# Two attention layers on one core: who rounds off B's v weights, and when the v stage's inputs are asked for

## The chip, the cores and the metric

The kernel runs on one core of one Trainium2 chip. The metric is the device time of one execution in microseconds (us); the median of three runs of the kernel before is 1763.21 us (1762.25 to 1763.91).

## The reference, cut to what matters

Two independent attention layers A and B read inputs of 2048 rows by 640 columns and share no data; their results stand side by side in the output.

```python
# both: H = 32 heads of Dh = 20, float32
qkv = (x @ wqkv).reshape(B, S, 3, H, Dh)          # q, k, v
# A: each row looks at itself and 7 earlier rows, 2 apart (W = 8, dil = 2)
logits = einsum("bhsd,bhswd->bhsw", q, kg) * scale ; attn = softmax(logits)
o = einsum("bhsw,bhswd->bhsd", attn, vg) ; a = o @ wo
# B: full attention, every row with every row
p = softmax(einsum("bhqd,bhkd->bhqk", q, k) * scale)
o = einsum("bhqk,bhkd->bhqd", p, v) ; b = o @ wo
return concatenate([a, b], axis=-1)
```

## The kernel before, in words

**Two parts for every operand.** TensorE multiplies rounded float32. To keep accuracy, each operand of a projection is split in two (`split`): a *first part*, the rounded value (ScalarE, ACT in the profile), and a *second part*, what rounding lost, by one subtraction (VectorE, DVE, unless another engine is passed as `second`). A product is three passes: first by first, first weight by second x, second weight by first x. So a matmul group can't begin its third matmul before the second part of its weights is there.

**Stages.** (1) A's q and k projections. (2) B's q and k projections: five loops over `m`, each with eight groups of 15 matmuls; the last one (`m == 8`, groups 0 to 7) is where the first inputs of the next stage are asked for. (3) The *v stage*: the v projections of A and then of B, in 15 blocks of four row tiles. x is held in eight columns (c = 0 to 3 of A, 4 to 7 of B) and the weights in two halves, so block 2c + half takes column c and one half. Blocks 0 and 1 are eight plain groups. From block 2 on a block is four *ticks*: 30 half-height matmuls for v and then four for one step of B's row maxima (`b_max`, scores into two PSUM pairs, each read by a VectorE maximum over 1024 columns). There are 52 such steps (`LEAD`). (4) The *loop*: 488 steps of B's attention, in which TensorE computes scores twice (transposed ones for the exponentials by ScalarE, plain ones for later maxima by VectorE) and multiplies by v. Its order is written out by hand in the string `ORDER`: S, Y, M and N are pairs of score matmuls with the PSUM banks they use, V ends a step, H is a piece of A's output projection, j a transposition for A. (5) 24 last steps without maxima, and B's output projection.

**A's attention** runs on GpSimd (POOL in the profile) beside all this, as a generator that hands out a few instructions per tick. `a_pace` lets it run until a running sum of estimated GpSimd time, `gp.us`, reaches a target; every `tensor_` operation given to `gp` adds to that sum, whoever gave it. The loop sets the sum to 0 and goes on at 2.4 us a step.

**What sets the order.** Each engine runs its own instructions in the order in which the program writes them; a waiting instruction holds up all behind it. All loads and stores named here are issued by SyncE (SP), in order. Buffers rotate: a load waits until the earlier use of its buffer is over. `stg` has three (weights before splitting), `p` six (x before splitting, and the B projections' results `pr` on their way to memory), `big` four (x columns, and `bk`, `bq`, the k and q of one group of B's heads), `w` four.

**The requests.** `wait[0]` holds after how many ticks a loaded piece is split. `x_pieces(xa, 0)` asks for x's first column of the v stage; `x_load(c, w)` for the later ones, with second parts by GpSimd; `wide_pieces(wv_a[1])` for A's second weight half, and `w_load(half, w)` for B's halves: half 0 after block 4, split nine ticks later (block 7's first tick), half 1 inside block 7, split four ticks later (block 8's second tick). In the profile these tiles are called `xn` and `xl` (x, four of five row chunks and the last), `ww` (weights), `stg` (what was loaded), `ro` (A's v on the way out), `ve` (B's), `mx` (maxima), `al`, `am`, `akv`, `aq`, `ao` (A's attention). Nearly every instruction shows line 71, that of a helper, so rows are told apart by tile.

## Time and profile before

| What | Value |
|---|---|
| Median of three runs | 1763.21 us |
| The profiled execution's own time | 1762.02 us |
| Its span, first to last instruction | 1760.2 us |
| Busy: TensorE, VectorE, ScalarE, GpSimd | 1734.1, 1357.8, 1338.2, 1265.9 us |
| Mean granted TensorE clock | 0.991 of full |

The span leaves 1.8 us of the execution's own time outside it. Stage 3 reaches from 280.85 us to about 469 us, the loop from there to about 1642 us. "Busy" of TensorE counts overlapping, modelled matmuls, so 99% says only that it rarely stood still for long; what a stage costs is read from the starts of its matmuls.

### The profile page before, as it was taken

How to read it: one execution, taken by the hardware profiler on the slowest of the kernel's cores; microseconds unless marked ns; L12 is line 12 of the kernel's file. 1: busy time of each engine (PE TensorE's matmuls, PEld its weight loads, DVE VectorE, ACT ScalarE, POOL GpSimd, SP SyncE). 2: the span in 40 equal slices, each digit the busy share in tenths (PEclk: the TensorE clock that was granted, in tenths of full speed). 3: DMA queues.
4: the chain of work that ended last, by engine and by line, in shares of the span. 5: the costliest groups of instructions: out<-in, count | busy, mean ns of one | idle time of the engine just before them, and what ended most of it. 6: DMA issues, size and time to landing. Idle time of an engine off the chain costs nothing.

```text
span 1760.2 us, 34683 instructions
## 1 busy us (share of the span) xinstructions
PE 1734.1 (99%) x12711; PEld 1014.8 (58%) x12711; DVE 1357.8 (77%) x1816; ACT 1338.2 (76%) x2658; POOL 1265.9 (72%) x1119
## 2 busy tenths in 40 slices
PE   9999998989999999999999999999999999999999
PEld 8988887979834544444354444444434444444569
DVE  3113232798899999999999999999989999999300
ACT  4223223231499999999999999999989999999881
POOL 0001940988899999999999999999999934544242
PEclk9999999999999999999999999999999999999999
DMA  6447868665755355445436344553553432111123
GB/s 224 121 142 251 301 224 273 210 200 168 207 175 136 110 128 163 129 116 152 138 110 154 115 135 114 168 157 103 141 151 116 119 83 58 44 36 52 33 71 115
DMA packets 194436, 248.29 MB, mean 141 GB/s; under 512 B 89309, under 2 KB 114397, under 8 KB 193273
## 3 DMA queue, kind: packets, MB, share of 16 engines
q1 hardware_dynamic: 193688, 245.41, 46.1%
q8 instruction: 100, 1.64, 0.4%
q10 hardware_dynamic: 576, 0.66, 0.1%
q14 instruction: 72, 0.58, 0.1%
HBM read 181.08 MB, written 64.91 MB: 140 GB/s over the span
## 4 chain that ended last, share of the span: by engine, by line
PE 77%; POOL 13%; DVE 5%; DMA 2%; ACT 2%; issue 2%; POOLq 0%; SPq 0%; DVEq 0%; ACTq 0%
PE ps_st L71 77%; POOL akv L71 7%; DVE mx L71 4%; POOL braw L71 3%; ACT e L71 1%; POOL ao L71 1%; DMA qb_d<-pr 1%; DVE ww L71 1%; POOL aot L71 1%; POOL al L71 0%; POOL ro L71 0%; DMA stg<-wv_a 0%; DMA stg<-xa 0%; DMA tr_d<-turn 0%; ACT more L71 0%
## 5 line engine op out<-in xcount | busy, mean ns | idle before, releaser
L71 DVE TENSOR_REDUCE mx<-ps_st 128x1 f32<-128x512 f32 (+1 forms) x1492 | 1226.7, 882 | 69.7 <-PE ps_st L71 58.8
L71 ACT ACTIVATE e<-ps_st 128x512 f32<-128x512 f32 x2048 | 1068.1, 629 | 33.5 <-PE ps_st L71 21.1
L71 PE MATMUL ps_st<-bk,bq 60*128 60x512 f32 x2048 | 561.8, 440 | 11.6 <-DVE mx L71 10.7
L71 PE MATMUL ps_st<-bq,bk 62*128 62x512 f32 x2048 | 548.2, 432 | 1.4 <-ACT e L71 1.3
L71 PE MATMUL ps_st<-e,vb 128*32 128x512 f32 x4096 | 545.0, 607 | 0.6
L71 PEld LDWEIGHTS ps_st<-bq,bk 62*128 62x128 f32 x2048 | 276.7, 185 | 402.8 <-ACT e L71 272.5
L71 POOL TENSOR_TENSOR braw<-braw,more 128x512 f32<-128x512 f32 x224 | 288.2, 1286 | 99.6 <-ACT more L71 99.0
L71 PEld LDWEIGHTS ps_st<-bk,bq 60*128 60x128 f32 x2048 | 258.3, 185 | 114.2 <-DVE mx L71 73.3
L71 POOL TENSOR_TENSOR akv<-akv,aq 128x1280 f32<-128x1280 f32 x64 | 188.5, 2945 | 166.2 <-DMA akv<-ka_d 166.1
L71 POOL TENSOR_TENSOR akv<-akv 128x640 f32<-128x640 f32 (+3 forms) x304 | 282.4, 929 | 14.9
L71 ACT COPY ro<-ps_st 128x320 f32<-128x320 f32 (+2 forms) x172 | 73.8, 465 | 190.3 <-PE ps_st L71 99.0
L71 PE MATMUL ps_st<-ww,xn 64*128 64x320 f32 (+1 forms) x1776 | 191.7, 315 | 7.4 <-ACT ww L71 4.8
L71 PEld LDWEIGHTS ps_st<-ww,xn 64*128 64x128 f32 (+1 forms) x1776 | 179.9, 192 | 24.2 <-ACT e L71 8.3
L71 PEld LDWEIGHTS ps_st<-e,vb 128*32 128x32 f32 x4096 | 82.5, 108 | 150.6 <-issue 76.8
L71 POOL TENSOR_TENSOR akv<-akv,al 128x1280 f32<-128x1280 f32 x64 | 151.5, 2367 | 0.1
L71 ACT COPY more<-ps_st 128x512 f32<-128x512 f32 x224 | 136.7, 610 | 4.0 <-PE ps_st L71 3.3
L71 PE MATMUL ps_st<-xn,w 128*128 128x512 f32 x480 | 115.8, 390 | 0.0
L71 POOL TENSOR_TENSOR xn<-stg,xn 128x512 fp32r<-128x512 f32 (+1 forms) x30 | 54.9, 1841 | 70.2 <-DMA va_d<-ro 62.9
L71 PEld LDWEIGHTS ps_st<-xn,w 128*128 128x128 f32 x480 | 90.1, 188 | 19.3
L71 PE MATMUL ps_st<-ww,aot 64*128 64x320 f32 x960 | 99.6, 309 | 0.0
L71 ACT CAST pr<-ps_st 128x512 fp32r<-128x512 f32 x40 | 23.5, 587 | 97.9 <-PE ps_st L71 95.0
L71 PEld LDWEIGHTS ps_st<-ww,aot 64*128 64x128 f32 x960 | 90.5, 186 | 4.9 <-issue 0.9
(65 smaller groups left out, 1046.0 us busy)
## 6 DMA issues: line engine op xcount, KB each, us to landing
akv<-ka_d SPq DMA_DIRECT2D x128, 320.0 KB
akv<-va_d SPq DMA_DIRECT2D x128, 320.0 KB
kb_d<-pr SPq DMA_DIRECT2D x20, 512.0 KB
qb_d<-pr SPq DMA_DIRECT2D x20, 512.0 KB
bk<-kb_d SPq DMA_DIRECT2D x16, 640.0 KB
bq<-qb_d SPq DMA_DIRECT2D x64, 160.0 KB
stg<-xb SPq DMA_DIRECT2D x16, 512.0 KB
rb<-s_d SPq DMA_DIRECT2D x128, 64.0 KB
```

The costliest lines, as they stand in the source:

```text
L71: return self.tc.keep_in_program_order(op(*a, **k))
```

## The change

Four edits, and a new `ORDER`:

- `w_load` passes GpSimd for the second parts of B's v weights; the first parts stay on ScalarE. Six VectorE instructions go, six GpSimd instructions come.
- x's first column is asked for in the loop `m == 6`, group 4, instead of `m == 8`, group 1: five groups sooner. It is split at the same tick as before (ten ticks after the request, not five).
- A's second weight half is asked for after group 3 of `m == 8`, not after group 7: four groups sooner, split at the same tick (seven, not three).
- x's second column is asked for after the first v group, not the second, and split one tick sooner.
- The `ORDER` string is another one throughout, with as many steps, H and j; S, Y, M and N are 627, 698, 444 and 127, where they were 619, 714, 452 and 111.

```diff
-    def wide_pieces(src, second=None):
+    def wide_pieces(src, second=None, first=None):
...
-            w[0][:, a:b], w[1][:, a:b], src[:, a:b], second=second, first=second and gp.tensor_copy) for a, b in PAIRS]
+            w[0][:, a:b], w[1][:, a:b], src[:, a:b], second=second, first=first or second and gp.tensor_copy) for a, b in PAIRS]
...
+                elif m == 6 and (n, j) == (2, 0):
+                    wait[0] = 10
+                    XV = [x_pieces(xa, 0)]
+                    for fn in XV[0][1]:
+                        fn()
+                    wait[0] = 2
                 elif m == 6 and (n, j) == (3, 0):
                     w0, loads = wide_pieces(wv_a[0])
                 elif m == 8:
                     g8 = 2 * n + j
                     if g8 == 1:
                         k_loads, q_loads = b_pieces(0)
-                        wait[0] = 5
-                        XV = [x_pieces(xa, 0)]
-                        for fn in XV[0][1]:
-                            fn()
                     elif 1 < g8 < 6:
                         k_loads.pop(0)()
+                        if g8 == 3:
+                            wait[0] = 7
+                            w1, more = wide_pieces(wv_a[1])
+                            for fn in more:
+                                fn()
                     elif g8 == 6:
                         for _ in range(4):
                             q_loads.pop(0)()
-                    elif g8 == 7:
-                        wait[0] = 3
-                        w1, more = wide_pieces(wv_a[1])
-                        for fn in more:
-                            fn()
...
-        WV[1][half], pieces = wide_pieces(wv_b[half])
+        WV[1][half], pieces = wide_pieces(wv_b[half], gp, act.copy)
...
-                if (block, s) == (0, 1):
+                if (block, s) == (0, 0):
                     x_load(1, 5)
...
-        "Y07S61M2Y45V0Y71S26M3Y05V7Y06M3S52Y71V0Y26M3S75VY71M5S24S03N17V2Y06S15Y34VM0S74Y56V3Y70S21N46VY70M4S12S63N07V1"
+        "Y07M1S36Y54V0Y71S26M4Y03V7Y06M4S31Y72V0Y13M4S76VY71M2S64S05N17V6Y04M2S51VY70M4S13S26N07V1Y25S04N36VY07S25M3Y61"
```

On SyncE, at the end of stage 2, the loads of A's second weight half (`stg<-wv_a`, its last three rows) stood so before, behind the last two of the first four loads of q (`bq`) and the last store of B's projections (`qb_d<-pr`):

```order
L71 DMA bq<-qb_d 20x1024
L71 DMA bq<-qb_d 40x1024
L71 DMA qb_d<-pr 128x2x512
L71 DMA stg<-wv_a 128x640 x2
L71 DMA stg<-wv_a 128x320
```

Now they stand so, right behind the second of the four loads of k (`bk`):

```order
L71 DMA bk<-kb_d 40x4096
L71 DMA qb_d<-pr 128x2x512
L71 DMA bk<-kb_d 22x4096
L71 DMA stg<-wv_a 128x640 x2
L71 DMA stg<-wv_a 128x320
```

The three loads have passed two loads of k, four of q and four stores of `pr`.

On GpSimd, in block 7, behind the x column of block 8 (`xn`, `xl`), A's attention (`akv`, `al`) came next before:

```order
L71 TENSOR_TENSOR xn<-stg,xn 128x1024 x2
L71 TENSOR_TENSOR xl<-stg,xl 128x512
L71 TENSOR_TENSOR akv<-akv 128x2x320
L71 TENSOR_TENSOR akv<-akv 128x2x160
L71 TENSOR_TENSOR akv<-akv 128x2x64
```

Now the two weight halves (`ww`) are there as well:

```order
L71 TENSOR_TENSOR xl<-stg,xl 128x512
L71 TENSOR_TENSOR ww<-stg,ww 128x640 x2
L71 TENSOR_TENSOR ww<-stg,ww 128x320
L71 TENSOR_TENSOR akv<-akv 128x2x320
L71 TENSOR_TENSOR akv<-akv 128x2x160
L71 TENSOR_TENSOR akv<-akv 128x2x64
L71 TENSOR_TENSOR akv<-akv 128x2x32
L71 TENSOR_TENSOR al<-akv 128x64
L71 TENSOR_TENSOR al<-al,am 128x256
L71 TENSOR_TENSOR akv<-akv,aq 128x1280
L71 TENSOR_TENSOR ww<-stg,ww 128x640 x2
L71 TENSOR_TENSOR ww<-stg,ww 128x320
```

Half 0 follows directly on the x column of block 8; half 1 comes after one more piece of A's attention, and ahead of block 10's column.

On VectorE, in blocks 5 to 9, the maxima (`mx`) had the two weight halves and a reciprocal for A (`am`) between them, and now follow one another:

```order
-L71 TENSOR_REDUCE mx_3092<-ps_st 128x2 x8
-L71 TENSOR_TENSOR ww<-stg,ww 128x640 x2
-L71 TENSOR_TENSOR ww<-stg,ww 128x320
-L71 TENSOR_REDUCE mx_3092<-ps_st 128x2 x10
-L71 TENSOR_TENSOR ww<-stg,ww 128x640 x2
-L71 TENSOR_TENSOR ww<-stg,ww 128x320
-L71 TENSOR_REDUCE mx_3092<-ps_st 128x2 x10
-L71 RECIPROCAL am<-am 128x32
-L71 TENSOR_REDUCE mx_3092<-ps_st 128x2 x2
+L71 TENSOR_REDUCE mx_3092<-ps_st 128x2 x30
```

Six subtractions have left VectorE, and the reciprocal comes later.

## The prediction

> **What bounds the kernel now.** I read the busy times first, then TensorE's own waits, then the starts of its matmuls where it waited, then what the named releasers did.

> ```profile
> PE 1734.1 (99%) x12711; PEld 1014.8 (58%) x12711; DVE 1357.8 (77%) x1816; ACT 1338.2 (76%) x2658; POOL 1265.9 (72%) x1119
> PE ps_st L71 <- DVE mx L71: 10.7, 7, 4.6
> PE ps_st L71 <- ACT ww L71: 4.8, 1, 4.8
> PE ps_st L71 <- POOL xn L71: 2.6, 2, 1.4
> ```

> The first row is busy time by engine, the others TensorE's waits (total, times, longest). TensorE hardly stands still: 18 us in three kinds of wait. Two of the kinds, and 7 of the 10.7 us behind the maxima, lie in the v stage, which is what the change touches. There TensorE alone sets the pace, so a wait counts in full, and more, as the starts of its matmuls show:

> ```profile
> 280.85 1.92 PE L71 MATMUL ps_st<-ww,xn 128*128 128x320 f32 x12
> 283.05 1.92 PE L71 MATMUL ps_st<-ww,xn 128*128 128x320 f32 x12
> ...
> 294.65 3.90 PE L71 MATMUL ps_st<-ww,xn 128*128 128x320 f32 x12 [4.83 <-ACT ww L71]
> ...
> 306.07 0.41 PE L71 MATMUL ps_st<-ww,xn 64*128 64x320 f32 x2
> ...
> 313.34 1.92 PE L71 MATMUL ps_st<-ww,xn 64*128 64x320 f32 x24
> ...
> 367.37 1.92 PE L71 MATMUL ps_st<-ww,xn 64*128 64x320 f32 x24
> ...
> 370.08 1.93 PE L71 MATMUL ps_st<-ww,xn 64*128 64x320 f32 x24
> ...
> 377.09 0.80 PE L71 MATMUL ps_st<-bk,bq 60*128 60x512 f32 x2 [4.64 <-DVE mx L71]
> ...
> 378.82 3.16 PE L71 MATMUL ps_st<-ww,xn 64*128 64x320 f32 x24
> ...
> 382.72 1.93 PE L71 MATMUL ps_st<-ww,xn 64*128 64x320 f32 x24
> ...
> 390.84 1.92 PE L71 MATMUL ps_st<-ww,xn 64*128 64x320 f32 x24
> ...
> 397.14 3.40 PE L71 MATMUL ps_st<-ww,xn 64*128 64x320 f32 x24
> ...
> 402.00 1.95 PE L71 MATMUL ps_st<-ww,xn 64*128 64x320 f32 x24
> ```

> An undisturbed group takes 283.05 - 280.85 = 2.20 us, an undisturbed tick 370.08 - 367.37 = 2.71. Against these, four places lose time:

> - A: blocks 0 and 1, eight groups from 280.85 to 306.07, take 25.22 where 8 x 2.20 = 17.6 would do: 7.6 lost, for a wait of 4.83. The rest is a slow clock: twelve matmuls take 3.90 behind the wait, not 1.92.
> - B: block 2's first tick, 306.07 to 313.34, takes 7.27, not 2.71: 4.6 lost, 2.6 of it waiting for x's second column.
> - C: from 370.08 to 382.72, two ticks take 12.64, not 5.42: 7.2 lost.
> - D: from 390.84 to 402.00, two ticks take 11.16: 5.7 lost.

> Together 25.1 us. This is what the change can win in the v stage, no more.

> **The change, part by part.** *A's second weight half, four groups sooner (place A).*

> ```profile
> 269.07 0.41 SPq L71 DMA_DIRECT2D bk<-kb_d  x1
> 285.72 3.66 SPq L71 DMA_DIRECT2D stg<-wv_a  x3
> 293.87 0.72 ACT L71 CAST ww<-stg 128x640 fp32r<-128x640 f32 x1 [7.99 <-DMA stg<-wv_a]
> 304.34 2.00 ACT L71 CAST xn<-stg 128x1024 fp32r<-128x1024 f32 x2
> 305.48 4.69 POOL L71 TENSOR_TENSOR xn<-stg,xn 128x1024 fp32r<-128x1024 f32 x2 [62.95 <-DMA va_d<-ro]
> 310.11 1.30 POOL L71 TENSOR_TENSOR xl<-stg,xl 128x512 fp32r<-128x512 f32 x1
> 250.00:265.00 15.00, 15.00 (x67) 12.36 (x67) 4.75 (x7) 4.68 (x8) 0.00 (x0) 1.00 0.62 209
> 265.00:312.00 47.00, 39.57 (x219) 35.41 (x219) 9.77 (x14) 13.26 (x24) 6.44 (x5) 0.90 0.83 271
> ```

> The loads are issued from 285.72 on and the first is rounded at 293.87, 8.15 us later, on queues that are 83% busy (last row: stretch, length, busy TensorE, its loads, VectorE, ScalarE, GpSimd, clock, DMA share, GB/s). Block 1 wants the weights at 280.85 + 4 x 2.20 = 289.65. Now they are issued behind the second load of k (269.07): about 269.5, and by the same 8.15 they are there at 278, some 8 us before ScalarE comes to them. The wait and its slow clock go: **-7.6**. Bounds: -4.8 (the clock stays slow) to -7.6; 0 if the loads don't come sooner (a rival).

> What the moved loads cost. The first load of k now waits longer, since x's column has taken the buffer that k had, and k gets that of the next B column: until group 3 of `m == 8` is done. Stores and the weights queue behind it on SyncE, for 1 to 2 us; TensorE has results in eight banks to write before that reaches it, so I cost it at nothing. x's first column goes from the busy stretch to the one before it (62% busy). Its three `p` buffers are held five groups longer, as they were from 265 to 280 before, without a wait of TensorE. Without that cover each late store would cost one group at most, 3.4 us.

> *x's second column, one group sooner (place B).* GpSimd begins at 305.48, behind ScalarE at 304.34, and ends at 311.4 (310.11 + 1.30); block 2 begins at 306.07. One group is 2.20 us, so against block 2 the column is ready 2.20 sooner: of the waits of 2.6, about 1.5 remain by the order of need (the second piece ends 1.0 late, the last 0.4). Behind a wait the clock stays slow: at C this cost 382.72 - 378.82 - 2.71 = 1.2, which I take. Lost 2.7 instead of 4.6: **-1.9** (0 if the load lands 2 us late, -4.6 at best). That the whole border is 1.31 MB lighter (x's first column has left it; at 271 GB/s 4.8 us) speaks for the load being in time.

> *B's weights by GpSimd (places C and D).*

> ```profile
> 369.60 6.30 DVE L71 TENSOR_TENSOR ww<-stg,ww 128x640 fp32r<-128x640 f32 x3
> 390.36 3.86 DVE L71 TENSOR_TENSOR ww<-stg,ww 128x640 fp32r<-128x640 f32 x3
> 265.16 0.83 DVE L71 TENSOR_TENSOR ww<-stg,ww 128x640 fp32r<-128x640 f32 x1
> 369.66 5.90 POOL L71 TENSOR_TENSOR xn<-stg,xn 128x1024 fp32r<-128x1024 f32 x2
> 376.99 3.41 POOL L71 TENSOR_TENSOR akv<-akv 128x640 f32<-128x640 f32 x4
> 381.44 2.96 POOL L71 TENSOR_TENSOR akv<-akv,aq 128x1280 f32<-128x1280 f32 x1
> L71 POOL TENSOR_TENSOR ww<-stg,ww 128x640 fp32r<-128x640 f32 x8 | 12.5, 1559 | 0.6
> L71 POOL TENSOR_TENSOR ww<-stg,ww 128x320 fp32r<-128x320 f32 x4 | 3.5, 872 | 0.3
> 395.00:400.00 5.00, 4.25 (x26) 3.65 (x28) 3.76 (x4) 1.40 (x2) 4.99 (x3) 0.52 0.15 53
> ```

> Before, VectorE takes 6.30 and 3.86 us for the halves, and the maxima behind them keep TensorE's banks: places C and D. Both go. What is late next is GpSimd: a half costs 2 x 1.56 + 0.87 = 4.0 us there. In the clock of the old trace: x's column for block 8 begins at 369.66 and, without VectorE beside it, takes 4.69 as at 305.48, and 1.30: 375.65. The pieces of half 0 end at 377.2, 378.8 and 379.6. Block 8 would begin at 370.08 + 2 x 2.71 = 375.5 and wants the first piece 0.3 later, the second 0.9 behind the first (30 matmuls in 2.20): waits of 1.4 and 0.7, then the slow clock, 1.2. C loses 3.3 instead of 7.2: **-3.9** (0 if GpSimd is 3 us later than in the old trace, -7.2 if TensorE is).

> Half 1: GpSimd does 7.4 us of A's work first (376.99 to 384.40), so its pieces end at 388.6, 390.1 and 391.0. Block 9 begins at 375.5 + 3.3 + 4 x 2.71 = 389.6 and wants them at 389.9, 390.5 and 391.4: in time, by half a microsecond. I leave 0.5 lost: **-5.2** (-2 to -5.7). SyncE, in turn, waits with half 1's loads until GpSimd frees `stg`, 3.7 us later than VectorE did; stores of A's v and the next x column are behind it, and both have a block's time. Later x columns have 4 us or more left on GpSimd by the same count.

> [...]

> *The loop.* It has the same matmuls, exponentials and maxima, differently paired.

> ```profile
> 468.00:1640.00 1172.00, 1167.12 (x8671) 531.41 (x8670) 1134.67 (x1577) 1133.29 (x2270) 1014.36 (x894) 1.00 0.42 120
> L71 DVE TENSOR_REDUCE mx<-ps_st 128x2 f32<-128x1024 f32 x556 | 671.9, 1217 | 42.7 <-PE ps_st L71 40.2 <-ACT e L71 0.5
> L71 DVE TENSOR_REDUCE mx<-ps_st 128x1 f32<-128x512 f32 x936 | 606.4, 683 | 26.9 <-PE ps_st L71 18.6
> DVE am L71 <- POOL al L71: 6.3, 3, 2.2
> 1310.00:1320.00 10.00, 7.35 (x44) 2.60 (x44) 7.62 (x10) 5.84 (x13) 9.76 (x10) 0.83 0.42 124
> ```

> VectorE and ScalarE are both busy for 97% of it, so it is their work that counts. M takes one maximum over 1024 (1.217), N two over 512 (0.683 each), Y one. Eight M fewer, 16 N more, 16 Y fewer: -9.7 + 21.9 - 10.9 = **+1.2**. GpSimd, which gave 8.0 us of the v stage to weights, does as much of A's attention later; it has room, since it is busy for 1014 of 1172 us. A new order can't win more than VectorE's idle 37 us; what it does to waits no row shows. I take none, and -4 to +8 for it.

> **Sum:** -7.6 - 1.9 - 3.9 - 5.2 + 1.2 = -17.4. The profiled execution's own 1762.02 becomes 1744.6; it lies 1.2 under the median of 1763.21, from which the forecast is **1745.8 us**.

> **The rivals.** *GpSimd bounds the v stage.* If it falls behind by 3 us more, C and D are given back almost whole, and B too: only A is won. 1763.2 - 7.6 + 1.2 = 1756.8. For it: GpSimd's work there grows by 8.0 while 17 us of TensorE's waits, in which it caught up, go. Against it: `a_pace` counts the weights and hands out less of A's work. [...] 0.12.

> *A's weights don't come sooner,* since SyncE is held by the load of k, or the queues stay full. A stays: 1745.8 + 7.6 = 1753.4. Against it: 8 us of slack. 0.06.

> *Slower: GpSimd's delay reaches VectorE in the loop.* At 1311 us VectorE waits 2.2 us for A's scores (`am` for `al`), and ScalarE loses 10 - 5.84 = 4.2 us between 1310 and 1320, while GpSimd is 98% busy. A's softmax comes 16 times; each further one that finds GpSimd late costs 4.2. From five on (1745.8 + 21 = 1766.8) the kernel is slower. Any other flaw of the new order that delays one step in a hundred by as much does the same. Against it: only three of 16 waited before, and the count of H and j falls two to three steps later in the new order, about the 8 us. 0.14, at 1768.

> *Better:* the stall at 1311 goes and the clock holds: 1745.8 - 4.2 - 2.4 = 1739. 0.10.

> **How the numbers follow.** Forecast 0.58, with its own range of 1741 to 1752; rivals 0.12, 0.06, 0.14, 0.10. From 1737 to 1759 some 0.82 of the chance lies; left out are the slower case and the ends. Within 0.2% (1759.7 to 1766.7, about what a measurement of this kernel can tell from no change) lie the near misses of two rivals: 0.07. Faster 0.80, slower 0.13.

> **What would show it.** Right: no wait for `ww` on ScalarE near 290; no wait for `mx` on TensorE in the v stage, but two of about 1 us for GpSimd's `ww` at block 8; the loop's first step some 18 us sooner than 469; 488 steps in 1172 to 1175 us. Wrong: waits for `xn` or `ww` of GpSimd over 3 us at blocks 8 to 14; a loop longer by over 8 us; more than three waits of `am` for `al`.

## The result, and the profile after

| | before | after |
|---|---|---|
| Median of four runs each | 1763.12 us | 1744.71 us (1743.93 to 1746.89) |
| Ratio, 95% interval | | 0.9898 (0.9881 to 0.9915): 1.0% less time, clear of the noise |
| Profiled execution, own time | 1762.02 us | 1745.1 us |
| Its span | 1760.2 us | 1742.9 us |
| Loop's first score matmul at | 468.95 us | 454.27 us |
| From there to the last stage (the loop) | 1175.20 us | 1173.76 us |
| The rest of the span | 116.05 us | 114.87 us |

The forecast of 1745.8 is 1.1 us from the median. That hides errors of about 5 us on opposite sides, which the rows below show.

Busy time by engine, after:

```profile
PE 1726.1 (99%) x12711; PEld 1011.2 (58%) x12711; DVE 1349.3 (77%) x1818; ACT 1337.3 (77%) x2658; POOL 1271.9 (73%) x1125
```

VectorE has 8.5 us less to do, GpSimd 6.0 more; neither sum says where the end moved. TensorE's waits over the whole span do (total, times, longest):

```profile
PE ps_st L71 <- ACT xn L71: 2.6, 2, 2.2
PE ps_st L71 <- POOL xn L71: 2.4, 2, 2.0
PE ps_st L71 <- DVE mx L71: 2.0, 5, 0.6
PE ps_st L71 <- POOL ww L71: 1.9, 3, 1.2
PE ps_st L71 <- ACT e L71: 1.8, 1, 1.8
```

The 4.8 us for ScalarE's `ww` are gone. The 10.7 behind VectorE's maxima are 2.0, all of them in the loop. New are 1.9 for GpSimd's `ww`, 2.6 for ScalarE's `xn` (2.2 of it in the v stage), of which no row of the profile before spoke, and 1.8 in one wait for ScalarE's `e`, in the loop. Where they lie is seen from TensorE's matmuls in the v stage (start, length, in brackets the idle time ahead and what ended it); the last two rows are the loop's first score matmul and the first matmul behind its end:

```profile
281.15 1.92 PE L71 MATMUL ps_st<-ww,xn 128*128 128x320 f32 x12
...
296.55 1.92 PE L71 MATMUL ps_st<-ww,xn 128*128 128x320 f32 x12
...
301.12 0.41 PE L71 MATMUL ps_st<-ww,xn 64*128 64x320 f32 x2 [2.21 <-ACT xn L71]
...
303.56 1.97 PE L71 MATMUL ps_st<-ww,xn 64*128 64x320 f32 x12 [2.02 <-POOL xn L71]
...
309.03 1.96 PE L71 MATMUL ps_st<-ww,xn 64*128 64x320 f32 x24
...
371.21 0.46 PE L71 MATMUL ps_st<-ww,xn 64*128 64x320 f32 x4
372.90 1.14 PE L71 MATMUL ps_st<-ww,xn 64*128 64x320 f32 x12 [1.23 <-POOL ww L71]
374.41 0.85 PE L71 MATMUL ps_st<-ww,xn 64*128 64x320 f32 x8 [0.37 <-POOL ww L71]
...
376.02 1.92 PE L71 MATMUL ps_st<-ww,xn 64*128 64x320 f32 x24
...
384.12 1.33 PE L71 MATMUL ps_st<-ww,xn 64*128 64x320 f32 x16
385.72 0.87 PE L71 MATMUL ps_st<-ww,xn 64*128 64x320 f32 x8 [0.27 <-POOL ww L71]
...
387.32 1.92 PE L71 MATMUL ps_st<-ww,xn 64*128 64x320 f32 x24
...
454.27 0.51 PE L71 MATMUL ps_st<-bq,bk 62*128 62x512 f32 x1
...
1628.03 1.92 PE L71 MATMUL ps_st<-e,vb 128*32 128x512 f32 x16
```

Read with the undisturbed 2.20 us a group and 2.71 a tick:

| Place | Lost before | Lost after | Change | Predicted |
|---|---|---|---|---|
| A, blocks 0 and 1: 296.55 - 281.15 = 7 x 2.20 | 7.6 | 0 | -7.6 | -7.6 |
| B, block 2's first tick: 309.03 - 298.75 - 2.71 | 4.6 | 7.6 | **+3.0** | -1.9 |
| C, block 8's first tick: 376.02 - 371.21 - 2.71 = 2.10 | 7.2 | 2.1 | -5.1 | -3.9 |
| D, block 9's first tick: 387.32 - 384.12 - 2.71 = 0.49 | 5.7 | 0.5 | -5.2 | -5.2 |
| Start of the stage: 280.85 became 281.15 | | | +0.3 | 0 |
| Loop, and the rest of the span (-1.4, -1.2) | | | **-2.6** | +1.2 |

(298.75 is where block 2 would begin: 296.55 + 2.20.) The rows of the table sum to -17.2; the span is 17.3 shorter.

Place B has got worse. What ScalarE did ahead of it, after:

```profile
294.37 0.43 ACT L71 COPY ro<-ps_st 128x320 f32<-128x320 f32 x1 [3.80 <-DMA va_d<-ro]
299.70 0.43 ACT L71 COPY ro<-ps_st 128x320 f32<-128x320 f32 x1 [4.90 <-DMA va_d<-ro]
300.02 1.99 ACT L71 CAST xn<-stg 128x1024 fp32r<-128x1024 f32 x2
```

ScalarE stands still for 3.80 and 4.90 us before a row copy (`ro`): it waits for the store of an earlier row (`va_d<-ro`) to free one of four row buffers. Behind the second copy, in ScalarE's order, stands the rounding of x's second column, at 300.02, though block 2 wanted it at 298.75. GpSimd's second parts follow only then, from 301.15. Before, with TensorE at rest at A and the stores going out meanwhile, ScalarE's last copy ahead of the column waited for TensorE only:

```profile
304.02 0.42 ACT L71 COPY ro<-ps_st 128x320 f32<-128x320 f32 x1 [1.78 <-PE ps_st L71]
304.34 2.00 ACT L71 CAST xn<-stg 128x1024 fp32r<-128x1024 f32 x2
```

So ScalarE, held by the store of a row, is the first wait at B, and GpSimd's second parts, which come after it, are the second. The stores did not move with the groups: SyncE issued the second row's store at 292.57 us, and before at 292.13, though its row was copied by 286.2 in both. SyncE issues in order, and ahead of that store stand two loads of q and the x column, the first of which was issued only at 289.62, after a wait of 3.2 us that the profile puts down to k's DMA (`bk`).

Two stretches of the loop, 200 us each, the first two rows of before, the other two of after (stretch, length, busy TensorE, its loads, VectorE, ScalarE, GpSimd, clock, DMA share, GB/s):

```profile
470.00:670.00 200.00, 199.85 (x1514) 96.12 (x1512) 194.22 (x285) 190.82 (x385) 189.11 (x168) 1.00 0.52 146
1270.00:1470.00 200.00, 196.66 (x1488) 90.34 (x1486) 190.86 (x266) 190.06 (x381) 159.82 (x135) 0.99 0.40 114
470.00:670.00 200.00, 197.08 (x1500) 91.21 (x1492) 193.12 (x280) 190.46 (x383) 191.97 (x172) 1.00 0.49 140
1270.00:1470.00 200.00, 199.83 (x1526) 93.98 (x1522) 196.39 (x278) 193.50 (x388) 158.34 (x135) 1.00 0.40 109
```

Before, the second stretch held the stall near 1311, and TensorE was busy for 3.2 us less in it than now: that stall is gone. In the first stretch TensorE is now busy for 2.8 us less. Most of this is one wait: ScalarE can't copy a partial result of B (`more`) until GpSimd has added an earlier one (`braw`), and TensorE then waits 1.85 us for ScalarE's `e`.

```profile
490.49 0.58 ACT L71 COPY more<-ps_st 128x512 f32<-128x512 f32 x1 [1.98 <-POOL braw L71]
```

The two nearly cancel. The loop's -1.4 is no more than the scatter: with the old `ORDER` and the same order of instructions the loops of before, e1 and e9 (below) take 1175.20, 1173.05 and 1174.54 us, and the seven kernels with the new `ORDER` in which `gp.us` counts B's weights take 1172.87 to 1174.89. The 1.2 us of the rest of the span come from a slow clock in before's profiled execution (0.50 of full from 1644.49 to 1647.90): there the second group of sixteen matmuls behind the loop starts 7.15 us after the first (1644.15, 1651.30), and in after 5.50.

### The profile page after: what moved, and what is told of

It is laid out like the page before. It is cut to its first block, busy times and chain, and to the rows that moved or that the text cites. A ratio compares the mean times of both kernels' runs of the same rounds, so it can differ in the third digit from the quotient of the medians.

```text
span 1742.9 us, 34666 instructions
## 1 busy us (share of the span) xinstructions
PE 1726.1 (99%) x12711; PEld 1011.2 (58%) x12711; DVE 1349.3 (77%) x1818; ACT 1337.3 (77%) x2658; POOL 1271.9 (73%) x1125
## 4 chain that ended last, share of the span: by engine, by line
PE 73%; POOL 17%; DMA 4%; issue 3%; DVE 2%; ACT 1%; SPq 1%; POOLq 0%; ACTq 0%; DVEq 0%
PE ps_st L71 73%; POOL akv L71 9%; POOL braw L71 4%; DVE mx L71 2%; POOL ao L71 1%; DMA stg<-xa 1%; SPq L71 1%; DMA mdr<-mtr 1%; DMA bq<-qb_d 1%; POOL ww L71 1%; POOL al L71 1%; ACT e L71 1%; DMA s_d<-braw 1%; POOL xn L71 0%; DMA s_d<-sm 0%
## 5 line engine op out<-in xcount | busy, mean ns | idle before, releaser
L71 DVE TENSOR_REDUCE mx<-ps_st 128x1 f32<-128x512 f32 (+1 forms) x1500 | 1227.5, 877 | 72.5 <-PE ps_st L71 61.4
L71 ACT ACTIVATE e<-ps_st 128x512 f32<-128x512 f32 x2048 | 1067.3, 630 | 32.5 <-PE ps_st L71 19.6
L71 PE MATMUL ps_st<-bk,bq 60*128 60x512 f32 x2048 | 555.1, 436 | 0.5 <-DVE mx L71 0.4
L71 PE MATMUL ps_st<-bq,bk 62*128 62x512 f32 x2048 | 548.7, 431 | 3.5 <-ACT e L71 1.8
L71 PE MATMUL ps_st<-e,vb 128*32 128x512 f32 x4096 | 543.1, 604 | 0.5
L71 PEld LDWEIGHTS ps_st<-bq,bk 62*128 62x128 f32 x2048 | 276.6, 184 | 401.6 <-ACT e L71 250.2
L71 POOL TENSOR_TENSOR braw<-braw,more 128x512 f32<-128x512 f32 x224 | 288.3, 1287 | 85.6 <-ACT more L71 85.1
L71 PEld LDWEIGHTS ps_st<-bk,bq 60*128 60x128 f32 x2048 | 257.9, 184 | 102.9 <-DVE mx L71 45.1
L71 POOL TENSOR_TENSOR akv<-akv,aq 128x1280 f32<-128x1280 f32 x64 | 188.4, 2944 | 166.4 <-DMA akv<-ka_d 166.3
L71 POOL TENSOR_TENSOR akv<-akv 128x640 f32<-128x640 f32 (+3 forms) x304 | 282.6, 930 | 14.7
L71 ACT COPY ro<-ps_st 128x320 f32<-128x320 f32 (+2 forms) x172 | 73.9, 465 | 185.9 <-PE ps_st L71 104.0
L71 PE MATMUL ps_st<-ww,xn 64*128 64x320 f32 (+1 forms) x1776 | 188.1, 311 | 6.5 <-POOL xn L71 2.4
L71 PEld LDWEIGHTS ps_st<-ww,xn 64*128 64x128 f32 (+1 forms) x1776 | 175.6, 187 | 22.6 <-ACT e L71 8.3
L71 PEld LDWEIGHTS ps_st<-e,vb 128*32 128x32 f32 x4096 | 82.2, 108 | 149.9 <-issue 77.1
L71 POOL TENSOR_TENSOR akv<-akv,al 128x1280 f32<-128x1280 f32 x64 | 151.6, 2368 | 0.1
L71 ACT COPY more<-ps_st 128x512 f32<-128x512 f32 x224 | 136.7, 610 | 4.0 <-POOL braw L71 2.0
L71 PE MATMUL ps_st<-xn,w 128*128 128x512 f32 x480 | 115.8, 390 | 0.0
L71 PEld LDWEIGHTS ps_st<-xn,w 128*128 128x128 f32 x480 | 90.1, 188 | 19.4
L71 POOL TENSOR_TENSOR xn<-stg,xn 128x512 fp32r<-128x512 f32 (+1 forms) x30 | 53.8, 1804 | 62.8 <-ACT xn L71 61.5
L71 PE MATMUL ps_st<-ww,aot 64*128 64x320 f32 x960 | 99.2, 308 | 0.0
L71 ACT CAST pr<-ps_st 128x512 fp32r<-128x512 f32 x40 | 23.5, 587 | 98.7 <-PE ps_st L71 93.0
L71 PEld LDWEIGHTS ps_st<-ww,aot 64*128 64x128 f32 x960 | 91.0, 186 | 4.6 <-DVE mx L71 0.5
```

The lines of the kernel that those rows point to most:

```text
L71: return self.tc.keep_in_program_order(op(*a, **k))
```

## The experiments

All times are medians, ratios against the kernel before on the same chip (1763.04 to 1764.22 there). "Start" and "loop" are those of the first table.

| Run | Median, us | Ratio (95%) | Start | Loop |
|---|---|---|---|---|
| e1, only the earlier requests | 1755.43 | 0.9955 (0.9937 to 0.9972) | 462.87 | 1173.05 |
| e2, only GpSimd | 1787.58 | 1.0137 (1.0121 to 1.0153) | 460.67 | 1211.06 |
| e3, all but the new `ORDER` | 1781.99 | 1.0108 (1.0085 to 1.0130) | 454.63 | 1209.29 |
| e4, only the new `ORDER` | 1763.95 | 0.9999 (0.9990 to 1.0008) | 467.73 | 1176.49 |
| e5, after + 7 row buffers | 1742.69 | 0.9880 (0.9865 to 0.9895) | 451.80 | 1172.87 |
| e6, after, x's second column late | 1747.52 | 0.9911 (0.9896 to 0.9926) | 454.47 | 1174.40 |
| e7, after, x's first column late | 1747.92 | 0.9913 (0.9897 to 0.9930) | 455.99 | 1174.89 |
| e8, e5 + column 2 by VectorE | 1737.60 | 0.9852 (0.9838 to 0.9867) | 447.08 | 1173.56 |
| e9, e3, GpSimd's work not charged | 1753.46 | 0.9948 (0.9931 to 0.9964) | 462.87 | 1174.54 |
| e10, before, charged | 1795.04 | 1.0189 (1.0171 to 1.0207) | 467.67 | 1210.76 |
| e11, after + column 2 by VectorE | 1742.99 | 0.9879 (0.9864 to 0.9894) | 450.43 | 1173.48 |
| e12, e8 + B's weights sooner | 1738.94 | 0.9857 (0.9840 to 0.9873) | 453.27 | 1173.95 |

### The parts alone (e1 to e4)

e1 and e3 start from the changed kernel, e2 and e4 from the kernel before:

```diff
e1  the changed kernel with the ORDER of before, and
-        WV[1][half], pieces = wide_pieces(wv_b[half], gp, act.copy)
+        WV[1][half], pieces = wide_pieces(wv_b[half])
e2  the kernel before, and
-        WV[1][half], pieces = wide_pieces(wv_b[half])
+        WV[1][half], pieces = wide_pieces(wv_b[half], gp, act.copy)
e3  the changed kernel with the ORDER of before
e4  the kernel before with the new ORDER
```

> Only the earlier requests, second parts of B's weights on VectorE, old ORDER. Theory (four local places in the v stage add up, the order string a little on its own): place A is gone (7.6 us), place B as in the changed kernel (7.6 lost, not 4.6), C and D as before (7.2 and 5.7). The loop's first score matmul stands at 468.95 - 7.6 + 3.0 = 464.4 us, the total is about 1758.5. Rival (the gain is the new order's): total within 1 us of 1763. Rival on B (the slow second column is caused by GpSimd's or the order's edits): B keeps its 4.6, first score matmul at 461.4.

> Only the second parts of B's v weights by GpSimd, old requests, old ORDER. Theory: C falls from 7.2 to about 2.1 and D from 5.7 to about 0.5, A and B as before (7.6 and 4.6): first score matmul at 468.95 - 10.3 = 458.7 us, total about 1752.8 with the old loop. Rival (GpSimd falls behind and pays in the loop under an order made for the old timing): stage as said, but a loop longer by 4 to 10 us, total 1757 to 1763.

> All edits of the changed kernel but the ORDER string, which is the old one. Theory: the v stage ends as in the changed kernel, first score matmul at 454.3 us; the loop is as long as before (1175.2 from the first score matmul to the first step without maxima), total about 1748. Rival (the old order does not fit A's later rows, which come two to three steps later): loop 5 to 15 us longer, total 1753 to 1763. Rival (the order string does nothing): total 1744.7 within 1.

> Only the new ORDER string, everything else as before. Theory: the v stage is that of before (first score matmul at 469.0 us), the loop and its end are about 3 us shorter as in the changed kernel: total about 1760. Rival (the gain is the new order's): total 1746 to 1750. Rival (each order fits only its own timing): loop longer than before's, total over 1763.

In the v stage the parts add up: the requests bring the start from 468.95 to 462.87 (-6.1), GpSimd to 460.67 (-8.3), both to 454.63 (-14.3). Not so in the loop. GpSimd's edit with the old `ORDER` makes it some 35 us longer (e2, e3), far beyond the 4 to 15 us that the rivals on record allowed, and those runs are slower than the kernel before. The new `ORDER` alone gains nothing: 1.3 us more loop, which is within the scatter, no change of the median, and not the 3 us less that were expected. That the parts add up, which e2 and e3 were to show, fell. In the prediction the new order was an edit with a price of its own; here it decides whether the kernel wins 1% or loses 1%.

e1 settles a rival about place B. Without GpSimd's edit and without the new order, block 2's first tick loses 308.94 - 298.85 - 2.71 = 7.4 us there, as in the changed kernel, so the earlier requests make B worse:

```profile
308.94 2.81 PE L71 MATMUL ps_st<-ww,xn 64*128 64x320 f32 x24
```

e1's start is 1.5 us sooner and its median 3 us lower than expected. C and D, left as they were, lost 8.3 and 2.0 us there, not 7.2 and 5.7; why was not followed.

### Why the old order costs 35 us (e9, e10)

Two theories. *Hand-out:* the subtractions given to `gp` add to `gp.us`, so `a_pace` hands out A's instructions later in the program; the old `ORDER` has its H (A's projection) and j (transposes) at fixed steps, and they no longer fit. *Lateness:* GpSimd really has 8 us more to do, and A's results come late on the chip. e9 keeps the work and takes away the charge; e10 keeps the work on VectorE and makes the charge.

```diff
e9  the changed kernel with the ORDER of before
+    class Uncharged:
+        def tensor_tensor(self, *a):
+            us = gp.us
+            gp.tensor_tensor(*a)
+            gp.us = us
...
+        WV[1][half], pieces = wide_pieces(wv_b[half], Uncharged(), act.copy)
e10  the kernel before
+    class Charged:
+        def tensor_tensor(self, *a):
+            gp.us += 0.2 + math.prod(a[0].shape[1:]) * 0.00212
+            return dve.tensor_tensor(*a)
...
+        WV[1][half], pieces = wide_pieces(wv_b[half], Charged())
```

> All edits of the change, the old ORDER, and the second parts of B's weights for v made by GpSimd but not charged to gp.us, the account by which A's instructions are handed out; TensorE's instructions then stand in before's own order through the whole loop, while GpSimd has 8 us more to do in the v stage. Theory (the 36 us of the run with all edits and the old ORDER came from the hand-out: A comes some steps later in the program, so that A's projection, the H tokens, is written out of its places): loop 1173 to 1178 us, median 1746 to 1751. Rival (GpSimd's own lateness holds up VectorE and ScalarE in the loop): the loop stays over 1200 us, median near 1780. Half of each: loop near 1190.

> The kernel before, in which the second parts of B's weights for v stay on VectorE, but gp.us is charged as if GpSimd made them: no engine has more or less to do, only A's instructions are handed out later against the old ORDER. Theory (the hand-out against the order is what costs): loop 1205 to 1215 us, median 1792 to 1802. Rival (GpSimd's own lateness): loop 1173 to 1178, median 1762 to 1766.

The hand-out it is: with GpSimd's work and no charge the loop takes 1174.54 us, with the charge and no work 1210.76. Counted in the program's order (steps by the products with v), before and e9 have A's projection as 32 groups of five chunks of six matmuls, never more than two chunks in a row without a score matmul. In e10 (and e3) eight of these groups stand as four of ten chunks each, without a score matmul between: the groups at the loop's 106th and 116th step come together at the 126th, those at 170 and 178 at 188, at 292 and 300 at 310, at 356 and 362 at 372. The code suggests why, which was not tried by itself: a j that finds no transpose ready passes, the transposes then wait until they fall due, 20 steps later, and H behind them.

On the chip, the kernel before, two chunks of one group and scores between them:

```profile
729.71 0.63 PE L71 MATMUL ps_st<-ww,aot 64*128 64x320 f32 x6
730.16 0.39 PE L71 MATMUL ps_st<-bk,bq 60*128 60x512 f32 x1
...
730.40 0.62 PE L71 MATMUL ps_st<-ww,aot 64*128 64x320 f32 x6
```

and e10's TensorE at one of its four places:

```profile
1238.94 4.67 PE L71 MATMUL ps_st<-ww,aot 64*128 64x320 f32 x60 [1.06 <-ACT e L71]
```

with its VectorE there:

```profile
1231.46 8.17 DVE L71 TENSOR_REDUCE mx<-ps_st 128x2 f32<-128x1024 f32 x9
1245.11 5.51 DVE L71 TENSOR_REDUCE mx<-ps_st 128x1 f32<-128x512 f32 x7 [5.48 <-PE ps_st L71]
```

Sixty matmuls in a row make no scores, and VectorE, busy for 97% of the loop before, stands still for 5.48 us. At the four places:

```profile
780.00:800.00 20.00, 18.24 (x152) 10.16 (x148) 13.24 (x19) 14.50 (x31) 19.53 (x20) 1.00 0.56 136
935.00:955.00 20.00, 18.64 (x158) 10.84 (x155) 13.57 (x18) 14.90 (x31) 17.83 (x19) 1.00 0.26 62
1230.00:1250.00 20.00, 18.94 (x162) 10.07 (x158) 14.15 (x20) 15.54 (x33) 19.43 (x21) 1.00 0.47 137
1390.00:1410.00 20.00, 18.08 (x140) 10.86 (x141) 11.75 (x18) 12.86 (x27) 15.94 (x14) 0.91 0.51 145
```

VectorE (the third of the counted busy times) is busy for 52.7 us of these 80; at the loop's 97% it would be for 77.5. So some 25 of e10's 35.6 lie here, worked out so. Compared with e9 step by step, by the starts of the products with v, it is 27.5 of 36.2: 7.0, 6.6, 5.6 and 8.4 us in the steps 120 to 140, 180 to 200, 300 to 320 and 360 to 380, which hold the four places. Another 5.0 lie in the first 40 steps, where ScalarE waits 1.87 us for GpSimd's `braw`, as in the changed kernel. That wait, 1.3 to 3.1 us, is in all ten kernels with the charge, e10 too, in which GpSimd makes no second parts of these weights, and in none of the four without it (before, e1, e4, e9): it too comes from the hand-out, and the new `ORDER` does not take it away. The rest was not followed to its places.

e9's median is 2.5 us above the range that the theory expected, though its loop is right: its start is 462.87, not 454.63. Without the charge `a_pace` hands out more of A's work beside the weights than with it. TensorE in e9's v stage:

```profile
414.69 0.50 PE L71 MATMUL ps_st<-bk,bq 60*128 60x512 f32 x2 [1.46 <-DVE mx L71]
...
416.15 2.94 PE L71 MATMUL ps_st<-ww,xn 64*128 64x320 f32 x24
```

and VectorE there:

```profile
412.88 0.62 DVE L71 TENSOR_REDUCE am<-al 128x32 f32<-128x256 f32 x1 [2.41 <-POOL al L71]
413.41 4.61 DVE L71 TENSOR_REDUCE mx<-ps_st 128x2 f32<-128x1024 f32 x4
```

VectorE waits 2.41 us for GpSimd's `al`, the maxima stand behind it, TensorE behind the maxima, and its next 24 matmuls take 2.94 instead of 1.92. Two ticks lose 4.1 us here (410.87 to 420.36); of the other 4, 3.1 lie at block 9, where e9 loses 3.6 (385.58 to 394.60) and e3 0.5. This is the chain of the "slower" rival, in the v stage. So charging the weights pays in the v stage, and needs an order made for it.

### Place B (e5, e8, e11)

Theory: ScalarE is held by the row copies, and GpSimd's second parts come after. Rival: GpSimd's second parts alone are too slow. e5 gives the first three rows of block 1 buffers that stand idle at that time (seven instead of four); e11 lets VectorE make the second parts of the second column; e8 does both.

```diff
e5  (a_row passes half == 1 and s < 3 as spare)
-    def store_rows(p, dst):
-        r = sb.tile([128, 320], F32, tag="r", bufs=4, name="ro")
+    def store_rows(p, dst, spare=False):
+        r = sb.tile([128, WA], F32, tag="ao", bufs=3, name="ro")[:, :320] if spare else sb.tile([128, 320], F32, tag="r", bufs=4, name="ro")
e11 (e8 is e5 and e11)
-        x, pieces = x_pieces((xa, xb)[c // 4], c % 4, gp)
+        x, pieces = x_pieces((xa, xb)[c // 4], c % 4, None if c == 1 else gp)
```

> The changed kernel with seven buffers, not four, for the v rows of blocks 0 and 1 on their way out (three of block 1's four take the idle ones of A's outputs). Theory 1 (at place B, ScalarE stands behind a row's copy that waits for one of four row buffers, whose stores come late on SyncE): ScalarE rounds the second column at about 294.8 us instead of 300.0, B loses 2.5 to 3.5 us instead of 7.6, first score matmul at about 450, total about 1740.5. Theory 2 (the second column's own load lands late, at about 300): B unchanged, first score matmul at 454, total 1744.7.

> As the run with seven row buffers, and the second parts of x's second column by VectorE, which has nothing to do there, not GpSimd. Theory 1: ScalarE rounds the column at about 294.8 us, VectorE ends 2.4 + 0.7 us behind it, B loses 0 to 1 us, first score matmul at about 447, total about 1737 to 1738 (beats both kernels). Theory 2: ScalarE still begins at 300, VectorE is 3 us faster than GpSimd, B loses 4 to 5, total about 1741.

> The changed kernel, and only the second parts of x's second column by VectorE in place of GpSimd; the four row buffers as they are. Theory (at block 2 the first wait is for ScalarE's first parts, late behind the row copies, and GpSimd's second parts come one behind the other after that): ScalarE's parts still come at 302 us, the wait of 2.2 us stays and the two for GpSimd go; block 2's first tick loses 4 to 6 us in place of 7.6, start of the loop 451 to 453, median 1741 to 1743. Rival (GpSimd's time for the second parts is the whole of it): the first tick loses under 2 us as in the version with both, start near 447, median 1738. Other rival (VectorE's second parts lengthen nothing here, but its maxima are held up later): no gain, 1744 to 1747.

With seven row buffers ScalarE's copies no longer wait for stores; in e5 the casts come 3.6 us sooner than in the changed kernel, and 1.6 later than expected, since they now wait for the column's loads:

```profile
296.42 1.05 ACT L71 CAST xn<-stg 128x1024 fp32r<-128x1024 f32 x1 [1.86 <-DMA stg<-xa]
```

Block 2's first tick then loses 4.1 us (305.10 - 298.33 - 2.71) instead of 7.6, what is left being two waits of 1.14 and 1.18 for GpSimd and the slow clock behind them (0.79 of full from 300 to 305 us, 0.87 from 305 to 310), which costs the second tick another 0.5:

```profile
305.10 2.48 PE L71 MATMUL ps_st<-ww,xn 64*128 64x320 f32 x24
```

With VectorE and four buffers (e11) it loses 3.7:

```profile
301.04 0.41 PE L71 MATMUL ps_st<-ww,xn 64*128 64x320 f32 x2 [2.08 <-ACT xn L71]
302.30 2.13 PE L71 MATMUL ps_st<-ww,xn 64*128 64x320 f32 x22 [0.85 <-DVE xn L71]
...
305.18 1.92 PE L71 MATMUL ps_st<-ww,xn 64*128 64x320 f32 x24
```

ScalarE's wait stays, GpSimd's two go. With both (e8):

```profile
298.20 1.48 PE L71 MATMUL ps_st<-ww,xn 64*128 64x320 f32 x14
300.06 1.00 PE L71 MATMUL ps_st<-ww,xn 64*128 64x320 f32 x10 [0.39 <-DVE xn L71]
...
301.80 1.93 PE L71 MATMUL ps_st<-ww,xn 64*128 64x320 f32 x24
```

1.0 is left (301.80 - 298.10 - 2.71). Both causes were there, of about equal size: each alone takes 3.5 to 3.9 us off the tick and brings the median to 1743 (with intervals that overlap the changed kernel's), both take 6.6 off it and bring the median to **1737.6**, clear of both kernels and the best version of this study. e8 and e11 also take these three subtractions out of `gp.us`; their loops, 1173.56 and 1173.48, show no harm from it.

### The requests one by one (e6, e7)

```diff
e6  the changed kernel
-                if (block, s) == (0, 0):
+                if (block, s) == (0, 1):
                     x_load(1, 5)
e7  the changed kernel: the branch in m == 6 goes, and in g8 == 1
+                        wait[0] = 5
+                        XV = [x_pieces(xa, 0)]
+                        for fn in XV[0][1]:
+                            fn()
```

> The changed kernel with x's second column asked for after the second group again, as before (edit undone). Theory 1 (row buffers): its loads no longer stand ahead of the second row's store on SyncE, so that store is out about 1.6 us sooner and the row buffers come free sooner, but the column is split one group later: B loses 5 to 8 us, near the changed kernel's 7.6; total 1742 to 1745. Theory 2 (the column's own load lands late): the load comes later still, B loses 9 to 10 us, total about 1747.

> The changed kernel with x's first column asked for in the last loop again, five groups later (edit undone). Theory (what the prediction said: moving this load takes 1.31 MB out of the full stretch, about 4.8 us of transfer): A's second weight half and the stores land 3 to 5 us later; the weights still come in time (A stays gone), B loses 2 to 4 us more than 7.6; total 1747 to 1749. Rival (the load is hidden anyway): total 1744.7 within 1.

Both medians are 3 us above the changed kernel's, but the intervals overlap. Neither shows a wait at A: its 7.6 us are the second weight half's alone. Both wait longer for ScalarE's `xn` at block 2: e6 for 3.61 us where after has 2.21, and e7 for 4.04. By the measure of the table B loses 8.3 us in e6 and 9.3 in e7, where after loses 7.6. So the earlier requests are worth 0.7 and 1.7 us at B, by one profiled execution each; e7's start comes 1.7 later, e6's 0.2 (454.47). e6 fell between its two theories; e7 lost a little less at B than its theory had (2 to 4). On the medians these runs leave it open. Since B stays as bad without either of them, what makes it worse than before is the third request, by which the stall at A goes; that one alone was not run.

### One more step (e12)

```diff
e12  e8, and
-            w_load(0, 9)
+            w_load(0, 7)
```

> The version with seven row buffers for block 1 and x's second column on VectorE, in which the parts of B's first half of weights for v are made two ticks sooner (wait 9 becomes 7), so that GpSimd makes their second parts ahead of those of x's fifth column. Theory: the two waits for ww at block 8 (1.25 and 0.37 us in that version) and with them some 2.1 us of the tick go, median 1735 to 1736.5. Rival: xn of the fifth column is now late by what GpSimd has in front of it, or A's next pieces are (am waits for al, mx behind it, TensorE behind that), and the time stays at 1737 to 1740.

No gain: 1738.94. The waits at block 8 are gone as the theory had it. At block 9 TensorE now waits 1.81 and 0.38 us for GpSimd's `ww`, where e8 waits 0.27. The wait has moved one block on, to half 1, which the rival did not name: GpSimd has the same work in front of half 1, only differently arranged. (e12's profiled execution lost 4.5 us at block 2 as well, where e8's lost 1.0 with the same code there, so its start of 453.27 is not e8's plus the edit; the profiled one is the longest of its four.)

## Why the prediction was right, and where it was not

- **Place A, -7.6: right.** The loads are issued at 269.83, the casts run without a wait, eight groups follow one another at 2.20 us.
- **Place B, -1.9: wrong, +3.0.** The step that failed: "One group is 2.20 us, so against block 2 the column is ready 2.20 sooner". It let x's column move with the groups. But removing A made block 2 begin 7.3 us sooner (306.07 became 298.75), and ScalarE, which rounds the column, came only 4.3 sooner (304.34 became 300.02): it stood behind row copies that waited for stores, and the stores went out no sooner than before (292.57 and 292.13 for the second row). The bounds (0 to -4.6) excluded a loss. e5, e8 and e11 show both parts of it, e6 that without the earlier request it would have been 0.7 worse. ScalarE's row copies had no place in the working, since no edit touched them; that the stall at A had given their stores the time was missed.
- **Place C, -3.9: too small, -5.1.** The two waits came as predicted in kind and order (1.23 and 0.37, for 1.4 and 0.7), but the slow clock behind them, 1.2 us, did not. Whether it comes is chance, as the last section shows: in e5, behind waits of 1.28 and 0.38 at the same place, it came, and the tick lost 3.4 (367.81 to 373.89), where 3.3 were predicted. **Place D, -5.2: right**, with 0.27 us of wait left.
- **Loop, +1.2: neither shown nor refuted.** It measured -1.4, and +1.3 in e4; loops with the same order of instructions differ by 2.1 us (before and e1). What the sum left out is larger than its term: the stall at 1311 goes (it stood among the rivals, as part of "better"), which is worth 3.2 in its stretch, and new waits, the longest one through GpSimd, take 2.8 back in another. The largest omission did not enter the sum: "what it does to waits no row shows. I take none". e2, e3 and e10 show that without the new order the charge on `gp.us` costs 35 us, through A's projection written out in blocks of ten chunks. The prediction mentioned that H and j fall "two to three steps later in the new order, about the 8 us", but used it only against a rival. "It has room, since it is busy for 1014 of 1172 us" reads a mean: up to 1270 us GpSimd is busy for 189.1 to 195.7 of every 200 us before, and the room comes after that.
- **The total** was right within 1.1 us by luck: B's error (+4.9) was offset by C's (-1.2) and by the loop's and the tail's (-3.8), of which no term of the sum was the cause. (A small slip: the waits behind the maxima in the v stage are 7.5 us by the profile, not 7.)
- **The rivals.** "GpSimd bounds the v stage" did not happen, as `a_pace` counts the weights: e9 takes that count away, and the start is 8 us later. "Slower" did not happen in the changed kernel: `am` waits for `al` twice, 3.5 us together, and never in the loop. GpSimd's delay does reach TensorE there once, through `braw` and ScalarE, for 1.85 us. The rival's chain is real, as e9 shows, and a flaw of the order worth 2% is real too, as e3 shows; both were avoided.

## What to carry to other kernels

A wait that you remove was also time in which something else, here the stores of rows, caught up: before you count the gain, list what every engine did during the stall and move the demands forward by it. Where work is handed out by an account and a hand-written order was fitted to that account, an edit to the account is an edit to the order: compare the places of the instructions with and without it before putting a price on either. And test the parts alone, with the account and the real work apart (e9, e10), since a total that fits can hide two errors of opposite sign.

## What the runs showed of the hardware that was not expected

```profile
298.85:302.26 3.41, 0.47 (x3) 0.19 (x2) 0.00 (x0) 2.56 (x4) 1.11 (x1) 1.00 0.76 271
302.26:309.09 6.83, 5.19 (x34) 4.59 (x36) 0.22 (x1) 0.93 (x3) 6.67 (x7) 0.50 0.89 316
...
372.33:375.74 3.41, 1.93 (x20) 1.36 (x18) 2.36 (x2) 1.07 (x3) 3.41 (x3) 1.00 0.13 16
375.74:379.15 3.41, 3.26 (x42) 3.18 (x44) 1.70 (x2) 0.92 (x2) 3.33 (x4) 1.00 0.81 263
385.99:389.40 3.41, 1.77 (x22) 1.47 (x22) 1.88 (x2) 2.23 (x4) 3.41 (x3) 1.00 1.02 351
389.40:392.81 3.41, 3.41 (x26) 3.22 (x26) 1.77 (x2) 0.43 (x1) 3.02 (x8) 0.50 0.54 192
```

In these traces the clock of a window goes with how busy TensorE was in the one before. At B of after the waits of 2.21 and 2.02 us left 0.47 us of work in one window, and two windows at half speed followed. In e11 waits of 2.08 and 0.85 us at the same place were parted by the border at 300.58 (1.80 us of work ahead of it, 2.10 behind it), and the clock stayed at 1.00. All windows of the 14 traces:

| Clock in the window | TensorE busy in it | Windows | Next one at 0.50 |
|---|---|---|---|
| 1.00 | under 50% | 26 | 26 |
| 1.00 | 50 to 90% | 131 | 18 |
| 1.00 | 90% and more | 6914 | 1 |
| 0.50 | under 87% | 19 | 19 |
| 0.50 | from 89.7% | 45 | 0 |

What decides between 50 and 90% these runs don't show. The longest wait in the windows shown above is 2.21 us. In a forecast the price of a slow clock behind a short wait is best given as a bound, since where the windows begin differs between executions: nothing, or up to half of 3.413 us, 1.7, for each window at half speed (an estimate from the lengths above).
